# A fused sparse-attention and ELU-MLP kernel: another opening order, earlier phase starts, and a later first local pair

## The chip, the core and the metric

The kernel runs on one core of a Trainium2 chip. The metric is device time in microseconds (us). The kernel before takes 330.13 us, the median of three runs (329.86 to 330.19). Engines are called PE (TensorE, matrix products and transposes), DVE (VectorE), ACT (ScalarE), POOL (GpSimd, which here mostly issues loads) and SP (SyncE, which issues output and transposing DMAs).

## The reference

Eight batches of eight heads, 576 positions of 64 columns. Heads 0 to 3 see the last 32 positions ("local"), heads 4 to 7 see the earlier positions with the same remainder by 32 ("strided"). The attention output, 4608 rows of 512, goes through two layers with an ELU between them.

```python
rel = pos[:, None] - pos[None, :]
mask_local = (rel >= 0) & (rel < 32)
mask_strided = (rel >= 0) & (pos[None, :] % 32 == pos[:, None] % 32)
scores = np.where(masks, q @ k.T / sqrt(64), -1e9)
attn = softmax(scores); x = attn @ v
h = x @ w_in                       # 512 -> 2048
g = np.where(h > 0, h, np.exp(np.minimum(h, 0)) - 1)
out = g @ w_out                    # 2048 -> 512
```

## The kernel before

**Staging.** Batch 0's attention is computed first, alone: the opening. Then come nine phases, `nb` = 0 to 8. Phase `nb` runs the MLP on chunk `nb` (512 rows) and, woven into it in phases 0 to 6, the attention of batch `nb + 1`. A phase has 16 slots `s`; each makes one 128-wide block of the first layer (`moe_in`, four 128x512 matmuls at L609), its activation (`moe_act`: an exponential on ACT at L635 into e_sb, then two DVE steps at L642 and L644 into g_sb), and one part of the second layer (`moe_out`, four matmuls at L654). Four parts make one output tile; the last copies the bank to o_sb on ACT (L658) and SP sends it out. From phase 1 on all these tiles share a single PSUM bank, so the first part of a tile can only start once o_sb of the tile before has been copied. A chunk's first three parts run in the last slots of its own phase, the other thirteen in the next one.

**Attention.** A batch has four pairs of heads: s0, s1 strided and l0, l1 local. A pair goes through `t_q` and `t_k` (q and k transposed on PE, L360 or L374, and copied out on ACT, L363 or L377; from batch 3, for local pairs from batch 4, by DMA instead), `scores(0)` and `scores(1)` (L491, for later batches L454; the exponential at L499, or L460 and L474, on ACT into pr; the mask on DVE at L506, or L462 and L477), `av(0)` and `av(1)` (pr times v at L526, divided on DVE at L534 and L535 into x), and `x_out` (x transposed on PE at L562 or L575 and copied into xT on ACT, or DVE for late local pairs, L569, L571, L579; a DMA for local pairs from batch 4). `v_in` (L413) copies a strided v into its layout, `halo` (L419) copies 32 rows of every local v block beside the next block, on DVE.

**Order.** The schedule is manual: each engine runs what the program emits, in that order. The opening's order is a written list, OPENING, with names such as `l0.a1` for av(1) of local pair 0; each `sN` step emits the scores, their exponential and their mask together. ON_VECTOR names the copies of batch 0 that go to DVE, the others go to ACT. Its last entries, `moe.2 moe.3 moe.0 moe.1`, are chunk 0's first three first-layer blocks, one contraction chunk after another (chunks 2 and 3 are the strided pairs). In the phases, TIMES gives per batch the first half-slot of pair 0, the pitch between pairs in half-slots, and the offsets of a pair's pieces from its own start; `attention` makes the table, and the slot loop runs the pieces that are due. Batches from 4 on take the local pairs first. In their phases (`late`) a slot's activation is emitted behind the pieces of its second half. PSUM banks come from rings: three single banks for transposes and AV results, two or three for first-layer blocks, a pair of banks for scores.

**Loads.** POOL issues them as a list: batch 0, w_in in four quarters, batch 1 between these, w_out, then later batches when buffers come free.

The slot loop's core (the lines that set what stands ahead of what on ACT):

```python
run(gaps, (2 * s,) if s else range(-10, 1))
late = EARLY <= nb + 1
if nb < n_chunks:
    moe_in(nb, s)
if nb < n_chunks and not late:
    moe_act(nb, s)
run(gaps, (2 * s + 1,) if s + 1 < MC else range(2 * s + 1, 1000))
if nb < n_chunks and late:
    moe_act(nb, s)
...
for chunk, i in outs(nb, s):
    moe_out(chunk, i)
```

## Time and profile before

| what | us |
|---|---|
| timed runs, median of 3 | 330.13 |
| the profiled execution | 333.11 |
| its span | 331.2 |
| PE busy in the span | 305.3 |
| DVE busy | 243.3 |
| ACT busy | 176.2 |
| POOL busy | 132.2 |

Durations in the text come from the profiled execution. 1.9 us of the execution lie around its span. By the order in time the opening lasts to about 29 us, phase 0 to about 58 and phase 1 to about 96; phases 2 to 6 take some 32 each, phases 7 and 8, without attention, less, and from 314 on there are only the last parts of the second layer. A row such as `164.98 1.02 PE L654 MATMUL ... x4 [0.44 <-ACT o_sb L658]` reads: start, duration, engine, line, operation, count, and in brackets how long the engine had stood idle and what released it. Line numbers are those of the kernel before.

### The profile page before, as it was taken

Reading aid. Unit: us, or ns where it says so; the run is one execution under the profiler, and the core shown is the slowest. Engines: PE = TensorE matmul, PEld = TensorE weight load, DVE = VectorE, ACT = ScalarE, POOL = GpSimd, SP = SyncE. Lnnn points to the kernel's source line nnn. Section 1 sums busy time; section 2 is a strip of 40 time slices with the busy share of each in tenths; the row PEclk is TensorE's granted clock in tenths of the full one; section 3 lists DMA queues with packets and bytes.
Section 4 is the critical chain, followed back from the end, with each engine's and each line's share of the span. In section 5 each row is a group of like instructions: output and inputs, shape, how many; then the busy total and the mean of one; then the engine's idle time right before and its main releaser. Section 6 shows DMA issues by size and latency. Waiting matters only on the chain.

```text
span 331.2 us, 6066 instructions
## 1 busy us (share of the span) xinstructions
PE 305.3 (92%) x2198; PEld 152.7 (46%) x2238; DVE 243.3 (73%) x540; ACT 176.2 (53%) x336; POOL 132.2 (40%) x208
## 2 busy tenths in 40 slices
PE   1787889999999999999999999999999999999992
PEld 1553554455544454445444444444445444444440
DVE  7584688788778878888788878887988566766600
ACT  3744787667545654556544555555455544344320
POOL 9859737857089479819921930000000000000000
PEclk9999699999999999999999999999999999999998
DMA  6999999999999999999989992920110000100012
GB/s 110 152 175 138 182 207 109 135 145 129 131 135 114 115 173 145 141 177 144 136 127 160 163 110 63 144 85 35 49 49 34 33 34 32 63 33 35 32 65 70
DMA packets 102138, 35.67 MB, mean 108 GB/s; under 512 B 79885, under 2 KB 97493, under 8 KB 102101
## 3 DMA queue, kind: packets, MB, share of 16 engines
q0 software_dynamic: 67632, 18.10, 60.0%
q1 hardware_dynamic: 34469, 17.11, 25.7%
q8 instruction: 19, 0.31, 0.4%
q14 instruction: 18, 0.15, 0.1%
HBM read 36.70 MB, written 9.44 MB: 139 GB/s over the span
## 4 chain that ended last, share of the span: by engine, by line
PE 80%; ACT 7%; DVE 5%; issue 3%; DMA 2%; POOL 2%; ACTq 0%; POOLq 0%; DVEq 0%
PE single L654 35%; PE half L609 27%; PE single L609 8%; PE single L526 3%; ACT e_sb L635 2%; DMA k_loc<-in_k_dram 2%; PE pair_a L454 2%; DVE g_sb L644 1%; PE single L374 1%; ACT xT L569 1%; PE single L562 1%; ACT pr L499 1%; ACT o_sb L658 1%; DVE e_sb L642 1%; PE pair_a L491 1%
## 5 line engine op out<-in xcount | busy, mean ns | idle before, releaser
L654 PE MATMUL single<-w_out_sb,g_sb 128*128 128x512 bf16 x559 | 143.6, 379 | 4.0 <-ACT o_sb L658 2.0
L609 PE MATMUL half<-xT,w_in_sb 128*128 128x512 bf16 x419 | 112.9, 387 | 1.4 <-issue 0.7
L635 ACT ACTIVATE e_sb<-half 128x512 f32<-128x512 f32 x109 | 65.6, 602 | 70.6 <-PE half L609 67.4
L642 DVE TENSOR_SCALAR e_sb<-e_sb 128x512 bf16<-128x512 f32 x139 | 61.7, 444 | 40.7 <-ACT e_sb L635 39.8
L654 PEld LDWEIGHTS <-g_sb 128*128 128x128 bf16 x576 | 53.4, 98 | 63.0 <-issue 3.4
L609 PEld LDWEIGHTS <-w_in_sb 128*128 128x128 bf16 x576 | 52.9, 100 | 57.6 <-issue 4.1
L644 DVE TENSOR_TENSOR g_sb<-e_sb,half 128x512 bf16<-128x512 bf16 x104 | 71.6, 688 | 3.6
L609 PE MATMUL single<-xT,w_in_sb 128*128 128x512 bf16 x134 | 36.8, 390 | 0.7 <-issue 0.5
L635 ACT ACTIVATE e_sb<-single 128x512 f32<-128x512 f32 x35 | 21.2, 605 | 20.6 <-PE single L609 18.9
L658 ACT COPY o_sb<-single 128x512 f32<-128x512 f32 x36 | 21.3, 591 | 16.9 <-PE single L654 16.4
L526 PEld LDWEIGHTS <-pr 128*128 128x128 bf16 (+3 forms) x352 | 21.3, 109 | 15.7 <-issue 3.2
L460 ACT ACTIVATE pr<-pair_a 126x936 bf16<-126x936 f32 (+1 forms) x20 | 19.2, 961 | 15.8 <-PE single L454 15.8
L177 POOL DMA_DIRECT2D v_raw<-in_v_dram x32 | 20.5, 685 | 17.9 <-DVE v_str L413 17.9
L177 POOL DMA_DIRECT2D k_str<-in_k_dram x32 | 20.1, 650 | 16.2 <-DMA k_loc<-in_k_dram 6.8
L644 DVE TENSOR_TENSOR g_sb<-e_sb,single 128x512 bf16<-128x512 bf16 x35 | 24.1, 688 | 1.2
L177 POOL DMA_DIRECT2D q_str<-in_q_dram x28 | 18.1, 675 | 6.0 <-DMA w_in_sb<-in_moe_w_in_dram 1.9
L535 DVE TENSOR_TENSOR x_l<-single,rden 96x384 bf16<-96x384 f32 x32 | 17.7, 554 | 1.1
L535 DVE TENSOR_TENSOR x_s<-single,rden 126x256 bf16<-126x256 f32 (+1 forms) x32 | 15.7, 491 | 1.1
L499 ACT ACTIVATE pr<-pair_a 128x576 bf16<-128x576 f32 (+2 forms) x20 | 13.0, 652 | 5.3 <-PE pair_a L491 5.2
L534 DVE RECIPROCAL rden<-single 96x6 f32<-96x6 f32 (+2 forms) x64 | 11.9, 185 | 2.8 <-PE single L526 2.4
L569 ACT COPY xT<-single 128x540 bf16<-128x540 bf16 x16 | 9.7, 608 | 7.1 <-PE single L562 7.1
L200 POOL DMA_DIRECT2D q_loc<-in_q_dram x16 | 12.5, 805 | 1.7 <-DMA v_raw<-in_v_dram 0.8
(111 smaller groups left out, 264.0 us busy)
## 6 DMA issues: line engine op xcount, KB each, us to landing
out_dram<-o_sb SPq DMA_DIRECT2D x36, 256.0 KB, 2.2
v_loc<-in_v_dram POOLq DMA_DIRECT2D x8, 288.0 KB, 8.6
k_str<-in_k_dram POOLq DMA_DIRECT2D x32, 67.5 KB, 4.4
v_raw<-in_v_dram POOLq DMA_DIRECT2D x32, 67.5 KB, 5.0
w_in_sb<-in_moe_w_in_dram POOLq DMA_DIRECT2D x4, 512.0 KB, 9.5
w_out_sb<-in_moe_w_out_dram POOLq DMA_DIRECT2D x4, 512.0 KB, 15.2
q_str<-in_q_dram POOLq DMA_DIRECT2D x28, 67.5 KB, 8.3
q_loc<-in_q_dram POOLq DMA_DIRECT2D x4, 288.0 KB, 5.7
```

The costliest lines, as they stand in the source:

```text
L177: engine.dma_start(out=t[0:108, h].rearrange("p g d -> p (g d)"), in_=rows[h, :, 0:30, :].rearrange("t (r g) d -> t r (g d)", g=5))
L460: nc.scalar.activation(both, sc[0:nk, :, 0:w], ACT.Exp, scale=scale)
L499: nc.scalar.activation(halves, sc[0:nk, :, 0:w], ACT.Exp, scale=scale)
L526: nc.tensor.matmul(av[0:m, p, blk - b0, :], lhsT=pr[0:nk, o:o + m], rhs=vt[0:nk, 2 * self.hp + p, blk, :], start=True, stop=True)
L535: nc.vector.tensor_tensor(self.x[0:nq, b0:b0 + n].rearrange("q g p d -> q p g d"), av[0:nq, :, 0:n, 0:D], r.unsqueeze(3).to_broadcast([nq, ...
L569: copy(rows[:, :, 0:30].rearrange("d t (r g) -> d t r g", g=5), groups[:, :, 0:108].rearrange("d g (t r) -> d t r g", r=6))
L609: nc.tensor.matmul(hps, lhsT=w_in_sb[:, c, m * 128:(m + 1) * 128], rhs=xT[:, c, nb * N_TILE:(nb + 1) * N_TILE], start=start, stop=stop)
L635: nc.scalar.activation(e_sb, hps, ACT.Exp)
L642: nc.vector.tensor_scalar(e1_sb, e_sb, scalar1=1.0, scalar2=1.0, op0=ALU.min, op1=ALU.subtract)
L644: nc.vector.tensor_tensor(g_of[nb][:, m, :], e1_sb, hps, op=ALU.max)
L654: nc.tensor.matmul(ops, lhsT=g_of[nb][:, m, kk * 128:(kk + 1) * 128], rhs=w_out_sb[:, m, :], start=(m == 0), stop=(m == MC - 1))
L658: nc.scalar.copy(o_sb, ops)
```

## The change

1. The opening list has another order. Masks are steps of their own (`m0`, `m1`), so a mask can stand behind other DVE work. The v copies stand ahead of the first local mask, the local scores ahead of the strided AVs, `moe.2` inside the local AVs, and q's transposes of batch 1's strided pairs (`S0.t_q`, `S1.t_q`) among the last steps; phase 0 leaves these two out.
2. Batch 0's halo copy goes from DVE to ACT.
3. Strided v of batch 1 is loaded ahead of its local q.
4. Batch 1 starts at half-slot 3 and not 4, batch 2 at 4 and not 6.
5. From batch 4 on, pair 0 (local) starts at half-slot 2 and not 1, with its av(1) where it was; the other pairs stay.
6. In late phases the last slot's activation is emitted ahead of the pieces left over.

```diff
-    (4, 6, (-3, -2, 0, 2, 4, 6, 9, 3)),
-    (6, 6, (-3, -2, 0, 2, 4, 6, 8, 0)),
+    (3, 6, (-3, -2, 0, 2, 4, 6, 9, 3)),
+    (4, 6, (-3, -2, 0, 2, 4, 6, 8, 0)),
     (2, 7, PIECES),
-    (1, 7, PIECES),
+    ((2, 8, 15, 22), 0, PIECES),
...
-s0.cast_q s0.t_q s0.t_k s1.cast_q s1.t_k s0.s0 s1.t_q s0.s1 l0.t_q s1.s1 s1.s0 l0.t_k
-l1.t_q l0.s0 s0.v l1.t_k s1.a0 s0.a0 l0.s1 s1.a1 s0.a1 l1.s0 l1.s1 s1.x s0.x s1.halo
-l0.a0 l0.a1 l1.a0 l1.a1 l0.x moe.2 l1.x moe.3 moe.0 moe.1
+s0.cast_q s0.t_q s0.t_k s1.cast_q s1.t_k s0.s0 s0.m0 s1.t_q s0.s1 s0.m1 l0.t_q s1.s1
+s1.m1 s1.s0 s1.m0 l0.t_k l1.t_q s0.v l0.s0 l0.m0 l1.t_k l0.s1 s1.a0 s0.a0 l0.m1 l1.s0
+s1.a1 s0.a1 l1.s1 l1.m0 s1.halo s1.x s0.x l1.m1 l0.a0 l0.a1
+l1.a0 moe.2 l1.a1 S0.t_q l0.x S1.t_q moe.3 l1.x moe.0 moe.1
...
     load_strided(1, "k")
+    load_strided(1, "v")
     load_local(1, "q")
-    load_strided(1, "v")
...
-                nc.vector.tensor_copy(t[0:32, :, 1:6, 0:D], t[96:128, :, 0:5, 0:D])
+                copy = nc.vector.tensor_copy if self.b else nc.scalar.copy
+                copy(t[0:32, :, 1:6, 0:D], t[96:128, :, 0:5, 0:D])
...
+            if self.b:
+                self.mask(u)
+        def mask(self, u):
...
+        begin = start if b >= EARLY else [start + pitch * i for i in range(4)]
         if b >= EARLY:
-            gaps[start] = [pairs[3].halo]
+            gaps[begin[0]] = [pairs[3].halo]
...
+            if b == 1 and pr.strided:
+                pr.t_q = lambda: None
...
-                               (at[5], lambda pr=pr: pr.av(1)),
+                               (at[5] - (b >= EARLY and i == 0),
+                                lambda pr=pr: pr.av(1)),
...
-                gaps.setdefault(start + pitch * i + off, []).append(piece)
+                gaps.setdefault(begin[i] + off, []).append(piece)
...
+    pairs.update((f"S{hp}", Pair(1, True, hp)) for hp in range(2))
...
-            late = EARLY <= nb + 1
+            late = EARLY <= nb + 1 and s + 1 < MC
```

More of the change, by code (lines that the diff above doesn't have):

```diff
@@ L499, in scores @@
             nc.scalar.activation(halves, sc[0:nk, :, 0:w], ACT.Exp, scale=scale)
+            self.pr[u] = pr
+            if self.b:
+                self.mask(u)
+        def mask(self, u):
+            nk, nq = self.blocks(u)[0][4:]
+            w = len(self.blocks(u)) // 2 * nq
+            halves = self.pr[u][0:nk, 0:2 * w].rearrange("k (a x) -> k a x", a=2)
             if not self.strided:
@@ L508, in scores @@
                                     op=ALU.mult)
-            self.pr[u] = pr
         def av(self, u):
@@ L545, in step @@
             elif what[1:].isdigit():
-                (self.scores if what[0] == "s" else self.av)(int(what[1:]))
+                {"s": self.scores, "m": self.mask, "a": self.av}[what[0]](int(what[1:]))
             else:
```

## The prediction

> **What bounds the kernel now.** I read the page's busy table first (TensorE, PE, is busy 92% of the span, no other engine over 73%), then PE's table of waits, then the order in time around each wait, and last PE's busy time in short windows with the clock that it was granted.

> ```profile
> PE single L360 <- ACT q_str L347: 3.6, 1, 3.6
> PE single L274 <- DVE key_q L272: 2.7, 1, 2.7
> PE single L654 <- ACT o_sb L658: 2.0, 5, 0.4
> PE pair_a L491 <- ACT kT_str L363: 1.1, 1, 1.1
> PE pair_a L491 <- ACT pr L499: 1.0, 2, 0.7
> ...
> PE single L374 <- ACT xT L571: 0.7, 2, 0.4
> ...
> PE single L575 <- DVE x_l L535: 0.7, 2, 0.5
> ```

> Columns: total us, times, longest. The first two are the first loads and the mask set-up, which the change leaves alone. Taken by window, all the rest but some 3 us lies before 58 us; from 58 us on PE hardly stops, and what it still waits for is one 0.51 at 93.96 and five waits for o_sb. So the end is set by PE; a wait of PE that goes shortens the run by its own length unless another takes its place.

> The late o_sb waits are one pattern, at 132.92, 164.98, 197.03 and 229.08, one for each of phases 3 to 6. PE, then ScalarE (ACT), start and duration in us:

> ```profile
> 162.64 1.04 PE L654 MATMUL single<-w_out_sb,g_sb 128*128 128x512 bf16 x4
> 163.51 1.03 PE L609 MATMUL half<-xT,w_in_sb 128*128 128x512 bf16 x4
> 164.98 1.02 PE L654 MATMUL single<-w_out_sb,g_sb 128*128 128x512 bf16 x4 [0.44 <-ACT o_sb L658]
> ```
> ```profile
> 162.70 0.97 ACT L460 ACTIVATE pr<-pair_a 128x960 bf16<-128x960 f32 x1 [0.85 <-PE single L454]
> 163.57 0.39 ACT L474 ACTIVATE pr<-single 128x96 bf16<-128x96 f32 x2
> 163.83 0.62 ACT L635 ACTIVATE e_sb<-single 128x512 f32<-128x512 f32 x1
> 164.31 0.62 ACT L658 COPY o_sb<-single 128x512 f32<-128x512 f32 x1
> ```

> The product that ends about 163.6 has its bank copied only at 164.31, because the exponentials of the local pair and an e_sb stand ahead of it. There is one such bank, so the next product stands still.

> The opening is different: PE is slow there as well as waiting. From the chain:

> ```profile
> 26.83 0.85 PE half L609 x2
> ...
> 57.47 0.86 PE single L654 x4
> ```

> Two 128x512 matmuls take as long as four do later: half pace until about 28.99. The clock column reads 1.00 there, but the pitch decides. It then reads 1.00 to about 32.4, 0.50 to about 39.2, and 1.00 after.

> **The change part by part.** The order of the changed program holds the same matmuls, copies and loads; they are moved, and one copy changes engine.

> *Late phases.* The first local pair's scores go behind the product whose bank is the only one. Replayed at phase 4: the first-layer matmuls end at 162.18, the product runs 162.18 to 163.05 and its last result is there at 163.2. ACT has e_sb until 163.0, so o_sb runs 163.25 to 163.85. Scores (0.4) and the next first layer (0.86) put the next product at 164.36: no wait, and 0.51 in hand. What is late next is the pair's chain: exponentials 163.75 to 165.0, masks on VectorE (DVE) to 165.6, its first AV product, also put later, due at 166.1. Slack 0.5. The last e_sb of each phase also passes ahead of the xT copies: they then end at 161.6, and the fourth matmul that reads them comes at 161.97; slack 0.35. On SP one 1.22 us transpose goes behind an output DMA; its result is read a phase later. So 4 x 0.44 = **-1.76**. Bounds: -2.2 (with the 0.1 holes near the scores) and 0.

> *Phase 1.* Batch 2 starts one slot (two half-slots, about 2 us) earlier, so its last transposes stand behind a product and not right behind the DVE that feeds them: **-0.51**. The cover is the loads: v of batch 2 has its last issue about 56.5 and lands 3.7 later, 60.2. Its copy on DVE now comes at 65.14; a slot earlier, and with 2.3 gained above it, 60.6. k lands about 56.5 and is due about 57.6. Cost 0, but every further gain above is paid back there, first as idle DVE. I keep +0.2 for it, bounds 0 and +1.

> *Opening, batch 0.* The v copies pass ahead of the first local mask, but they can't start before v has landed: last issue 9.32 plus 6.1, 15.4; the first AV goes from 16.25 to about 15.85. Local scores 1 pass ahead of the AVs, so ACT's last exponential ends about 18.85 and not 19.74. The halo copy leaves DVE (0.49, 20.64 to 21.13) for ACT, where no row of before has it. ACT's v_str rows take 0.62 for 512 and 0.83 for 768 columns; the line through both gives 1.28 for its 1280. Bounds 0.83 and 1.45, their sum. It waits for v_loc (landed 18.55), which costs nothing now, and ends 20.1 where DVE's ended 21.13. Behind it on ACT stand the four strided xT copies, at 0.7 a pair: 20.8 and 21.5 where they ended 20.4 and 21.1. Local AV 2 and 3 wait for those banks, so the 1.0 gained at the halo shrinks to about 0.6 at local AV 3 (21.5).

> *Opening, q of batch 1.* Ten transposes and two ACT copies of 0.68 come forward into the stretch where ACT waits 4.17 us (24.5 to 28.6). q's loads, last issue 15.9, landing 6.5 to 8.0 later, are in by 22.4 to 23.9; the first use is about 23.5. On PE they stand ahead of products that were back to back and cost 2 x 0.55 at half pace. From 21.85, 12 dense products at 0.43, these 1.1, two local transposes of 0.48 and an AV of 0.36 are 7.6, so the stretch ends at about 29.4 where it ended 29.25. The opening itself gains nothing.

> What follows it does. Before:

> ```profile
> 28.64 0.60 ACT L635 ACTIVATE e_sb<-half 128x512 f32<-128x512 f32 x1 [4.17 <-PE half L609]
> 29.57 0.68 ACT L363 COPY qT_str<-single 128x630 bf16<-128x630 bf16 x1 [0.33 <-PE single L360]
> 30.15 0.69 ACT L363 COPY kT_str<-single 128x630 bf16<-128x630 bf16 x1
> ...
> 33.82 0.60 ACT L635 ACTIVATE e_sb<-half 128x512 f32<-128x512 f32 x1 [0.88 <-PE half L609]
> 34.32 1.35 ACT L413 COPY v_str<-v_raw 126x512 bf16<-126x512 bf16 x2
> ```

> Without the q copy the k copy ends at 30.35, not 30.84, and the scores and all behind them move 0.5. The v copies now stand ahead of the e_sb that waited 0.88 for PE: they start about 32.4, not 34.32, and the AV that waits for them about 33.1, not 34.98: **-1.9**, carried on because PE is the slow one to 39 us. From 39 to 57 us PE waits 0.39, 0.16, 0.30, 0.34 and 0.16; the half-slot earlier start and the xT copies behind a first layer attack these, but DVE is over 90% busy from 40 to 50 us, so I take **-0.4** of the 1.35. Together -2.3, bounds +2 and -3.8.

> *Loads.* v of batch 1 is issued 0.7 earlier, local q 3.1 later (from 23.84 to 26.9, landing 5.7 after at 32.6; first use about 39). POOL holds the same list, so later loads keep their place: 0.

> **Sum** against the profiled execution, 333.11 us with a span of 331.2: -1.76 - 0.51 - 2.3 + 0.2 = -4.4, that is 328.7. The median of the timed runs is 330.13, 2.98 less than the profiled one; I take the same 4.4 off it: **325.7**.

> **The clock.** In windows of 3.41 us the 128x512 matmuls kept PE busy 1.49 (to 25.58: pace stayed half), 3.41 (to 28.99: it rose), 0.54 (to 32.4: it fell), 1.39 (stayed half), 2.44 (rose), 1.57 (stayed full). So it rises somewhere between 1.49 and 2.44, and falls between 1.57 and 0.54. Transposes and short matmuls alone held PE busy 3.07 of the 3.41 us to 11.93, and the pace stayed half. [...]

> **Rivals.**
> - *The clock holds.* In the window to 32.4 the changed order has about 1.14 us of these matmuls, between 0.54 and 1.57. If that is enough, the half-pace stretch goes, and the sixth first-layer block moves by 3.2 and not 1.9: 325.7 - 1.3 = 324.4. Against: the loads of batch 2 then bind. 0.17.
> - *The early gain is lost.* ACT carries halo, xT and q copies in a row; any one late holds PE in order, and DVE may stall for v at 60.2. With nothing left of it, 330.13 - 1.76 - 0.51 = 327.9; at the bad bound, +2, 329.9. 0.18, a third of it at that bound.
> - *The late wait changes place.* The xT copies miss their 0.35 or the masks their 0.5, and each phase pays back 0.44: 325.7 + 1.76 = 327.5. 0.07.
> - *Slower: the clock is late.* The ten transposes split the dense products; if the window that should raise the clock holds under some 2 us of them, PE enters phase 0 at half pace, and there first layers are 5.2 of 9.7 us, 1.8 in 3.41: perhaps too few to rise. A three-slot cycle then takes 9.7 and not 5.7, +4. From about the second cycle (clock still half after 43 us) the run is slower: 330 to 334. Against: by my replay the window to 28.99 holds 2.9. 0.10.
> - Forecast 0.48, by itself 324.8 to 326.8.

> **How the numbers follow.** A measurement of this kernel tells about 0.2%, 0.66 us. Faster: 0.48 + 0.17 + 0.07 + 0.12 of the lost gain = 0.84. Same: 0.05, slower 0.01 of the lost gain; slower 0.10 + 0.01. The range 324.2 to 329.0 leaves out the slow clock and the bad bound.

> **What would show it.** PE's wait for o_sb falls from 2.0 to about 0.2, the 0.51 near 94 is gone; first scores of batch 1 near 30.4 and their AV near 33.1; the halo on ACT about 1.3 long, ending near 20.1, the local AV just behind it. Wrong: a new wait of PE for xT or pr in phases 3 to 6, DVE waiting for v_raw near 60, half clock after 39 us.

## The result, and the profile after

The changed kernel takes **327.56 us** (median of four runs, 326.01 to 327.67) against 330.16 for the kernel before on the same chip; ratio 0.9893, 95% interval 0.9851 to 0.9934. Run again later, it took 327.1 against 331.27 (ratio 0.9892, 0.9854 to 0.993). The medians differ by 2.6 and 4.2 us; both ratios say some 3.5, with an interval of 2.2 to 4.9. The forecast was 325.7, with a range of 324.2 to 329.0: the direction and the range held, and by the first median 1.9 of the 4.4 us that it promised did not come. As 4.4 lies inside the interval, where the forecast failed is to be seen in the parts and not in the whole.

PE's table of waits in the profile of after (span 325.9; its execution took 327.67), the six rows behind its first two (the first loads and the mask set-up, which are as before, 3.7 and 2.7):

```profile
PE single L622 <- DMA w_in_sb<-in_moe_w_in_dram: 1.4, 1, 1.4
PE single L584 <- DVE x_l L544: 0.8, 1, 0.8
PE pair_a L493 <- ACT kT_str L364: 0.8, 1, 0.8
PE pair_a L493 <- ACT pr L501: 0.7, 1, 0.7
PE single L535 <- DVE pr L516: 0.7, 1, 0.7
PE half L622 <- DVE g_sb L657: 0.5, 1, 0.5
```

The wait for o_sb, five times before, is not in the table any more. The first two rows here stand in phase 0 and are new there: weights of the first layer that have not landed, and an x_l that VectorE has not divided. (Lines moved with the change: L622 is the first layer, L667 the second, L671 the copy to o_sb, L493 and L501 the scores and their exponential, L535 the products with v, L584 and L571 the transposes of x.)

Phase 4 around the place where PE stood still for 0.44 us, first PE, then ACT (start and duration in us):

```profile
159.62 1.03 PE L667 MATMUL single<-w_out_sb,g_sb 128*128 128x512 bf16 x4
160.58 0.39 PE L456 MATMUL pair_a<-qT_loc,kT_loc 64*128 64x96 bf16 x10
...
160.94 1.04 PE L622 MATMUL half<-xT,w_in_sb 128*128 128x512 bf16 x4
161.82 1.03 PE L667 MATMUL single<-w_out_sb,g_sb 128*128 128x512 bf16 x4
```
```profile
160.69 0.59 ACT L671 COPY o_sb<-single 128x512 f32<-128x512 f32 x1 [0.27 <-PE single L667]
161.17 0.98 ACT L462 ACTIVATE pr<-pair_a 128x960 bf16<-128x960 f32 x1
```

The copy now runs ahead of the pair's exponentials, right behind its product, and ends at 161.28; the next product comes at 161.82 and waits for nothing. This is the order that the prediction replayed.

The opening and phase 0, PE, from four places in time:

```profile
28.86 0.28 PE L493 MATMUL pair_a<-qT_str,kT_str 64*128 64x126 bf16 x4 [0.78 <-ACT kT_str L364]
...
31.81 0.35 PE L535 MATMUL single<-v_str,pr 126*128 126x65 bf16 x4 [0.69 <-DVE pr L516]
...
42.03 1.04 PE L622 MATMUL single<-xT,w_in_sb 128*128 128x512 bf16 x4 [1.43 <-DMA w_in_sb<-in_moe_w_in_dram]
...
54.60 0.30 PE L584 MATMUL single<-identity,x_l 96*128 96x96 bf16 x3 [0.81 <-DVE x_l L544]
```

The first scores of batch 1 come 2.0 us earlier than before (30.89) and their products with v 3.2 earlier (34.98). But the first o_sb copy comes only 1.5 earlier (58.73 after 60.24). Half of what the opening wins is gone again within phase 0.

A table for the whole text. Each profile is cut at five landmarks; "opening" runs from the first transpose of x_s to the products of batch 1's first pair with v, "phase 0" from there to the first o_sb copy, "phase 1" to the fifth, "rest" to the last. The kernels in the lower rows are those of the experiments.

| kernel | opening | phase 0 | opening + phase 0 | phase 1 | rest |
|---|---|---|---|---|---|
| before | 16.30 | 25.26 | 41.56 | 36.65 | 228.32 |
| late_only | 14.16 | 23.92 | 38.08 | 37.05 | 225.89 |
| early_only | 12.99 | 25.88 | 38.87 | 35.59 | 228.02 |
| after | 13.11 | 26.92 | 40.03 | 36.50 | 225.35 |
| after_again | 13.66 | 25.99 | 39.65 | 35.62 | 225.39 |
| loads_back | 14.06 | 26.73 | 40.79 | 35.59 | 225.45 |
| b2_at6 | 13.00 | 25.62 | 38.62 | 36.58 | 225.58 |
| win2_early | 13.92 | 27.63 | 41.55 | 35.59 | 225.49 |
| sq_back | 13.69 | 26.99 | 40.68 | 35.59 | 226.17 |
| hold | 13.80 | 25.84 | 39.64 | 35.95 | 225.70 |
| b1_at4 | 14.35 | 25.13 | 39.48 | 35.59 | 225.73 |
| b1_at4_win2 | 14.71 | 25.14 | 39.85 | 36.37 | 226.30 |
| halo_dve | 12.09 | 26.21 | 38.30 | 36.48 | 225.34 |
| best | 13.54 | 24.80 | 38.34 | 36.35 | 225.80 |

Two things show how far one profile can be trusted. After, after_again, early_only and b2_at6 run the same program as far as the first o_sb copy, and opening and phase 0 take 38.62 to 40.03 there; the twelve kernels with the late half have 225.34 to 226.30 as "rest". And look at the first two rows: late_only runs the same program as before until phase 3 begins, and yet opening and phase 0 are 3.5 us shorter in its profile. The profile of before, on which the prediction was built, showed the pace at half from 32.4 to 39.2; that of late_only has full pace there. The mean granted clock of every run tells how often: 10 of 66 runs of the kernel before had 0.986 or 0.987 (as the profiled one had) and took 333.2 us in the median; the other 56 had 0.994 or more and took 330.2.

### The profile page after: what moved, and what is told of

Same layout as the page of the kernel before. It is cut to its first block, busy times and chain, and to the rows that moved or that the text cites. A ratio compares the mean times of both kernels' runs of the same rounds, so it can differ in the third digit from the quotient of the medians.

```text
span 325.9 us, 6073 instructions
## 1 busy us (share of the span) xinstructions
PE 302.3 (93%) x2198; PEld 151.5 (46%) x2238; DVE 242.9 (75%) x539; ACT 177.7 (55%) x337; POOL 131.8 (40%) x208
## 3 DMA queue, kind: packets, MB, share of 16 engines
q1 hardware_dynamic: 34469, 17.11, 25.6%
## 4 chain that ended last, share of the span: by engine, by line
PE 77%; DMA 14%; POOL 4%; issue 1%; DVE 1%; ACT 1%; POOLq 0%; DVEq 0%; ACTq 0%
PE single L667 36%; PE half L622 25%; PE single L622 9%; DMA w_out_sb<-in_moe_w_out_dram 6%; DMA q_loc<-in_q_dram 4%; DMA w_in_sb<-in_moe_w_in_dram 3%; PE single L535 3%; PE pair_a L456 2%; DMA v_raw<-in_v_dram 2%; PE single L375 1%; POOL k_str L178 1%; PE single L571 1%; POOL v_raw L178 1%; POOL q_str L178 1%; PE pair_a L493 1%
## 5 line engine op out<-in xcount | busy, mean ns | idle before, releaser
L667 PE MATMUL single<-w_out_sb,g_sb 128*128 128x512 bf16 x557 | 143.4, 379 | 1.5 <-DVE g_sb L657 0.4
L622 PE MATMUL half<-xT,w_in_sb 128*128 128x512 bf16 x420 | 111.3, 382 | 1.7 <-DVE g_sb L657 0.5
L667 PEld LDWEIGHTS <-g_sb 128*128 128x128 bf16 x576 | 53.5, 98 | 59.5 <-DVE g_sb L657 1.0
L622 PEld LDWEIGHTS <-w_in_sb 128*128 128x128 bf16 x576 | 52.2, 99 | 58.1 <-issue 2.2
L622 PE MATMUL single<-xT,w_in_sb 128*128 128x512 bf16 x135 | 36.1, 382 | 2.0 <-DMA w_in_sb<-in_moe_w_in_dram 1.4
L648 ACT ACTIVATE e_sb<-single 128x512 f32<-128x512 f32 x35 | 21.0, 601 | 23.2 <-PE single L622 21.1
L671 ACT COPY o_sb<-single 128x512 f32<-128x512 f32 x36 | 21.2, 588 | 17.7 <-PE single L667 17.1
L535 PEld LDWEIGHTS <-pr 128*128 128x128 bf16 (+3 forms) x352 | 21.5, 108 | 16.7 <-DVE pr L516 1.7
L178 POOL DMA_DIRECT2D q_str<-in_q_dram x28 | 18.2, 695 | 5.6 <-DMA w_out_sb<-in_moe_w_out_dram 2.0
L501 ACT ACTIVATE pr<-pair_a 128x576 bf16<-128x576 f32 (+2 forms) x20 | 13.0, 652 | 5.4 <-PE pair_a L493 5.4
L201 POOL DMA_DIRECT2D k_loc<-in_k_dram x16 | 12.4, 783 | 1.6 <-DMA q_loc<-in_q_dram 1.3
```

Source lines behind the costliest of these rows:

```text
L178: engine.dma_start(out=t[0:108, h].rearrange("p g d -> p (g d)"), in_=rows[h, :, 0:30, :].rearrange("t (r g) d -> t r (g d)", g=5))
L201: nc.gpsimd.dma_start(out=t[:, h // 2, 0:4, h % 2], in_=src[name][b, h, 0:512].rearrange("(i p) d -> p i d", p=128))
L501: nc.scalar.activation(halves, sc[0:nk, :, 0:w], ACT.Exp, scale=scale)
L535: nc.tensor.matmul(av[0:m, p, blk - b0, :], lhsT=pr[0:nk, o:o + m], rhs=vt[0:nk, 2 * self.hp + p, blk, :], start=True, stop=True)
L622: nc.tensor.matmul(hps, lhsT=w_in_sb[:, c, m * 128:(m + 1) * 128], rhs=xT[:, c, nb * N_TILE:(nb + 1) * N_TILE], start=start, stop=stop)
L648: nc.scalar.activation(e_sb, hps, ACT.Exp)
```

## The experiments

Theory A is the prediction's sum: the late half (items 5 and 6 of the change) is worth 1.8 us, the early half (items 1 to 4) 2.6, and they add. Theory B: the early half gives back what it wins, to loads and to chains on VectorE and ScalarE that the earlier start does not move. Theory C: the clock decides, by where its windows fall.

### The two halves: late_only and early_only

late_only is the kernel before with items 5 and 6 alone; early_only is the changed kernel without them:

```diff
-    ((2, 8, 15, 22), 0, PIECES),
+    ((1, 8, 15, 22), 0, PIECES),
...
-                               (at[5] - (b >= EARLY and i == 0),
+                               (at[5],
...
-            late = EARLY <= nb + 1 and s + 1 < MC
+            late = EARLY <= nb + 1
```

> The kernel before with the late phases' part alone (first local pair a half-slot later, last activation ahead of the left-over pieces). Theory: each of phases 3 to 6 loses its whole gap between the starts of two products, 0.61 (164.98 against 164.37), not the 0.44 shown as idle, and the last one also the 0.28 by which a group of four products stretched to 1.30 at 258.33: 4 x 0.61 + 0.28 = 2.7 us less, no wait for o_sb above 0.2. Rival (as predicted): 4 x 0.44 = 1.76 less. Second rival: most of the gain of the whole change is elsewhere, under 1 us less here.

> The whole change without its late part (items 5 and 6 undone). Theory: what is left is the opening and phases 0 and 1, 1.9 us less than before in the profile up to the end of phase 2, with the four waits for o_sb back. Rival: the early part's gain in the one profile came from where the clock's windows fell, and the timed runs show between 0 and 1 us less.

late_only took 329.36 against 330.05 (ratio 0.9959, 0.9921 to 0.9997), early_only 329.16 (0.9954, 0.9923 to 0.9985). The product of the ratios, 0.9913, agrees with the whole change within the intervals: nothing speaks against the halves adding. In late_only five of twelve runs had a granted clock of 0.985 or 0.986 (median 330.8); the seven others, 0.994 to 0.999, took 328.2. In the same comparison the kernel before took 329.9 at such clocks and 333.2 in its five runs at 0.986 or 0.987, so the late half is worth 1.7 and 2.4. early_only is 0.9 less than the kernel before by the medians of all runs and 1.5 by the ratio (0.5 to 2.5); the forecast had 2.6 for it. In early_only's profile the old wait stands in each of phases 3 to 6, at 129.61, 161.67, 193.72 and 225.77; here the second:

```profile
160.20 1.03 PE L622 MATMUL half<-xT,w_in_sb 128*128 128x512 bf16 x4
161.67 1.02 PE L667 MATMUL single<-w_out_sb,g_sb 128*128 128x512 bf16 x4 [0.44 <-ACT o_sb L671]
```

The late half is thus all that it was said to be, and more: "rest" goes from 228.32 to 225.89 in late_only and from 228.02 to 225.35 in after, 2.4 to 2.7 and not 1.76 (1.7 to 3.0 with the spread of "rest" above). The rows show why. Start to start it is 161.67 - 160.20 = 1.47 where such a group without a wait takes 0.86, so each wait cost 0.61; the 0.44 in brackets leaves out the last 0.17 us of the 1.03 for which the group ahead is counted as busy. Four of them are 2.4, as late_only's theory had it. The early half is what came out small.

### Parts of the early half: loads_back and b2_at6

loads_back is the changed kernel with item 3 undone; b2_at6 has batch 2 at half-slot 6 again:

```diff
     load_strided(1, "k")
-    load_strided(1, "v")
     load_local(1, "q")
+    load_strided(1, "v")
```
```diff
-    (4, 6, (-3, -2, 0, 2, 4, 6, 8, 0)),
+    (6, 6, (-3, -2, 0, 2, 4, 6, 8, 0)),
```

> The whole change, with batch 1's loads in the old order (local q ahead of strided v). Theory: the new order makes the last load of w_out wait for local q (1.59 on POOL at 35.77), and with it every later load comes some 3 us late; undone, PE's 1.43 wait for the third quarter of w_in and DVE's 2.8 wait for v of batch 2 go, and the run is 1 to 2 us shorter than with the whole change. Rival: these loads are late because transfers from 25 to 30 us were slow for another reason (the rate there was 74 to 124 GB/s against 140 to 164 before); then both waits stay and the time is the same within 0.5.

> The whole change, with batch 2 started at half-slot 6 as before. Theory: started at 4, DVE stood 2.8 us for v of batch 2 and PE 0.54 behind it; at 6 that wait is under 1 and PE's 0.54 goes, but the 0.5 wait of the last local transposes for DVE at the end of phase 1 comes back, so the time is within 0.7 of the whole change. Rival: the earlier start is worth its 1.3 us (the step of the output copies between the fourth and the fifth), and the run is over 1 us longer.

loads_back took 326.73 (ratio 0.9885, 0.9832 to 0.9939), no different from the changed kernel. The wait for the weights is gone from its profile, and another has come:

```profile
PE single L535 <- ACT v_str L414: 1.4, 1, 1.4
```

So in these two profiles item 3 moves the weights back and v forward by about the same: the two waits change places (1.43 for 1.43). The wait for the weights does not come with the new order each time, though: early_only, sq_back and hold have that order and no such wait. The prediction's 0 for the loads is right as a sum and wrong in its reason ("later loads keep their place"). DMA moved 83 and 105 GB/s in the two halves of the stretch from 27 to 31 us in after and 165 and 128 in loads_back. Over the whole stretch it is 84 to 114 in after, after_again, early_only, b2_at6, win2_early, sq_back and hold, which have both strided loads back to back, and 141 to 154 in before, late_only and loads_back, where a local load stands between them. That the loads behind come later for this reason is a reading; no run singles it out.

b2_at6 took 327.87 (ratio 0.9923, 0.9894 to 0.9953), 0.3 to 0.8 more than the changed kernel, which the intervals alone do not tell apart. Its wait for x_l at the end of phase 1 is 0.5 again, and phase 1 takes 36.58, as before. Of the eleven profiles with batch 2 at 4, seven take 35.59 to 35.95 there. The other four, after, b1_at4_win2, halo_dve and best, take 36.35 to 36.50; in after VectorE waits 2.80 for v of batch 2, in best 2.1. So the step was named rightly and is worth about 1.0, and nearly nothing where v comes late.

b2_at6 also measures the opening and phase 0 by themselves, as beside late_only nothing else differs in it, in one comparison: 327.87 against 329.36, so 1.5 less. Among runs with clocks of 0.994 or more it is only 0.5 (327.7 against 328.2). The rest comes from executions at a low clock: 15 of 78 runs of the two kernels with the old opening had 0.985 to 0.987, but only one of 86 runs of the kernels with a new one. Which of its moves does that isn't shown.

### The clock's windows and single moves: after_again, win2_early, sq_back, hold

win2_early issues the last quarter that phase 0 waits for ahead of batch 1's local loads. sq_back puts batch 1's strided q back into phase 0. hold adds nine products whose results nobody reads, three at each of three idle places:

```diff
+    load_w_in(2)
     load_local(1, "q")
...
-    load_w_in(2)
```
```diff
-l1.a0 moe.2 l1.a1 S0.t_q l0.x S1.t_q moe.3 l1.x moe.0 moe.1
+l1.a0 moe.2 l1.a1 l0.x moe.3 l1.x moe.0 moe.1
...
-            if b == 1 and pr.strided:
-                pr.t_q = lambda: None
```
```diff
+    def fill(n, bank):
+        for _ in range(n):
+            nc.tensor.matmul(bank, lhsT=w_in_sb[:, 0, 0:128], rhs=w_in_sb[:, 0, 0:512],
+                             start=True, stop=True)
...
+            if (self.b, self.name) == (1, "s0"):
+                fill(3, coming())
...
+            if (self.b, self.name, u) == (1, "s0", 0):
+                fill(3, coming())
```

> The changed kernel once more, beside the next three on one chip. The theory that the two halves of the change add: late half -1.9, early half -0.9, so 327.3 against 330.1 and a ratio near 0.992. The rival that the halves help each other (the first run of the changed kernel, 327.56, by luck on the slow side): 326.5 or less. In its profile the late half should show at every late phase again (the start of the copy of the late products 0.6 earlier per phase), and the opening may come out up to 1.5 us otherwise than in the first profile, since the transfers of its first 30 us do not land alike in two executions.

> The last load of the first weights (the one that the products at 42.03 waited 1.43 us for) is issued ahead of the local loads of batch 1 instead of behind them; nothing else differs from the changed kernel. Theory that the load order cost the early half its gain: the wait of 1.43 goes, the local loads of batch 1 land some 2 us later and are used late enough, so -1.0 to -1.4 us against the changed kernel of the same call. Rival: the time comes back at the next wait in line (the activation of the half, 0.54 at 66, or the local values of batch 1, which the run with the old load order waited 1.4 for): within 0.5 of the changed kernel. Slower by up to 1 would mean that the local loads of batch 1 were the tighter ones.

> The transposes of batch 1's strided q go back to phase 0; the rest is the changed kernel's, the order of the opening too. In the changed kernel's first profile these ten transposes took 0.53 us of TensorE's time at 23.9 to 25.3 and lay in the window that ended at 25.14 with 3.12 of 3.41 us busy, after which the granted clock was 1. Theory that all of TensorE's busy time counts in that window: without them it holds some 2.6, the clock rises one window later, at 28.5, and the nine dense products of the opening that ran in 0.4 to 0.6 us take 0.63; the first scores of batch 1 come 1 to 1.5 us later than 28.86, and the two heads' transposes fall into idle time of phase 0 (0.78 at 28.1, 0.69 at 29.1), which gives some 0.5 back: +0.5 to +1 us in all. Rival, the reading of the prediction that only the dense products count: the rise stays where it is and the kernel is the same or up to 0.5 faster, as the transposes then lie in idle time.

> Nine products of 128x512 whose results nobody reads are added, three each ahead of the first two scores and of the first products with the values of batch 1, where TensorE stood idle for 0.78, 0.69 and 0.69 us in the window from 28.56 to 31.97 (1.68 us busy, after which the granted clock fell to half for one window of 3.41 us). At full clock three take some 0.66 us of TensorE. Theory that the busy share of that window decides: with them it holds some 3.4, the clock stays, and the 3.41 us of work at half clock that followed take 1.7 less; the added products cost at most 0.3 where they outlast the idle time: -1.0 to -1.5 against the changed kernel of the same call. Rival: the work behind that point is bound by its loads (the wait of 1.43 at 42.03 for the weights grows by what is gained), so the time is the same within 0.4 and the wait for the weights shows 2.5 to 3. Third: the clock falls as before whatever is added, and the nine products cost up to 0.7.

In one comparison: after_again, the changed kernel once more, 327.1, win2_early 327.83, sq_back 328.18, hold 327.69, against 331.27 (ratios 0.9892, 0.9905, 0.9918 and 0.9902, each about 0.004 either way). None of the other three is faster than the changed kernel. The two theories of after_again, 327.3 where the halves add and 326.5 or less where they help each other, are too near for it to tell.

- *win2_early.* The wait for the weights is gone, and nothing is won: as the rival had it, the time comes back at the next wait, though not at one that it named. Phase 0 takes 27.63. The transposes of x_s now wait 1.06 for VectorE, and the window of 3.41 us that holds this idle time (2.05 busy) is followed by one at half pace, from about 44.6:

```profile
43.66 0.32 PE L571 MATMUL single<-identity,x_s 108*128 108x108 bf16 x3 [1.06 <-DVE x_s L544]
...
44.29 1.57 PE L622 MATMUL half<-xT,w_in_sb 128*128 128x512 bf16 x4
```

- *sq_back.* About 1 us slower by the median, as expected, and for another reason: the clock did not rise late (the dense products moved up into the place of the transposes, and the window to 25.6 was full, 3.41 us), but ACT had to copy q and k in a row, and the first scores of batch 1 waited 1.58 for kT_str, not 0.78. The move of these ten transposes into the opening is thus worth about 1, if the difference is real: the intervals of the two ratios overlap.
- *hold.* It tells nothing of the clock: after_again, which has no added products, kept full pace through the same place, where its windows cut the three idle times differently (2.48 and 2.40 us busy, where the first profile had 2.94 and 1.68). What the added products cost, if anything, lies within the 0.6 by which the two differ.

### The earlier start and the halo: b1_at4, b1_at4_win2, halo_dve

```diff
-    (3, 6, (-3, -2, 0, 2, 4, 6, 9, 3)),
+    (4, 6, (-3, -2, 0, 2, 4, 6, 9, 3)),
```
```diff
-                copy = nc.vector.tensor_copy if self.b else nc.scalar.copy
+                copy = nc.vector.tensor_copy
```

The first is b1_at4; b1_at4_win2 adds win2_early's edit to it; the second is halo_dve.

> Batch 1 starts at half-slot 4 of phase 0 again, as it did before the change, so its pieces stand behind the other half of each slot; the rest is the changed kernel's. Between its first products with the values of batch 1 and the first copy of the late products the changed kernel took 25.99 to 26.92 us in its two profiles, where the kernel with the late half alone took 23.92: the waits there are for the weights (0.95 to 1.43), x_s (0.3 to 0.8), x_l (0.8) and pr (0.3 to 0.5), none of which the kernel before has. Theory that the earlier start itself makes them, since every piece is asked for some 0.9 us sooner than VectorE, ScalarE and the weights can give it: with the old start these waits fall from 2.5 to under 1, the stretch takes about 24.5, and as it begins about 0.9 later the whole comes out 0.3 to 0.8 faster than the changed kernel (326.9 to 327.6), near 326.5. Rival: the earlier start was worth its half-slot and the waits come from elsewhere: 0.5 to 1 slower, near 328.

> The old start of batch 1, and besides the last load of the first weights issued ahead of batch 1's local loads. Theory that the two waits are separate: the wait for the weights is gone and so are those for x_s and x_l; 0 to 0.5 faster than with the old start alone. Rival, that with the old start the weights are in time anyway (they land about 42 and would be asked for at 41.5): within 0.3 of it, or slower by what the local loads then come late (first used about 37).

> The halo copy of batch 0 is made by VectorE as before the change; the rest is the changed kernel's. In all profiles of the changed opening the time from the first x_s transpose to the first dense product is 3.58 to 3.59 us, in the two of the old opening 4.91. Theory that the halo on ScalarE (1.27 us there, 0.49 on VectorE) is where most of that 1.32 comes from: with it on VectorE, TensorE waits some 0.5 for it again and the stretch takes 4.1 to 4.6, +0.3 to +0.8 on the whole if it is carried on. Rival, that the order did it (the exponentials and masks ahead of it): VectorE makes the halo in 0.5 us and ScalarE starts the xT copies 1.2 earlier, the stretch takes 3.2 to 3.6 and the whole is the same or up to 0.4 faster.

b1_at4 took 327.12, b1_at4_win2 327.23, halo_dve 326.47, against 330.92 (ratios 0.9877, 0.9882, 0.9877; 0.005 either way). b1_at4 shows what its theory said of the waits: those for the weights, for x_s (0.2 left) and for x_l are gone, phase 0 takes 25.13. (Waits for pr, which it counted too, are no mark of the earlier start: late_only has 1.2 of them, b1_at4 1.0.) But v is waited for 1.33, PE is busy for 1.43 of the 3.41 us to 32.81, and after that the pace is half. All six timed runs seem to have that stretch (granted clock 0.990 to 0.992 in each): 3.41 us at half clock lower the mean of a span of 325 us by 0.005. Of the 0.008 that this profile's 0.992 is short, 0.003 are left, and where they lie is not shown; in before and after the clock column also falls at the idle end of the span, to 0.50 for the last 1.2 us and to 0.78 for the last 0.9. b1_at4_win2 is the same within the noise: with the old start the weights are in time.

halo_dve goes to the rival: the time from the first x_s transpose to the first dense product is 3.09 with VectorE's copy (3.21 in best, which has it too), 3.58 to 3.89 with ScalarE's, 4.91 before. The order of the opening won that stretch, and the halo's move to ScalarE (1.27 us there) lost some 0.5 of it.

### All that helped together: best

The changed kernel with batch 1 at half-slot 4, the halo on VectorE, and eleven unread products (three, three and five) in the idle times of 0.78, 0.69 and 1.33.

> The changed kernel with batch 1 at half-slot 4, the halo copy of batch 0 on VectorE, and eleven products of 128x512 whose results nobody reads (three ahead of each of the first two scores of batch 1, five ahead of its first products with values), which fill the idle times of 0.78, 0.69 and 1.33 us there. With batch 1 at half-slot 4 alone all six timed runs had a mean granted clock of 0.990 to 0.992, where most runs of the other changed kernels have 0.994 to 0.999, and the profile shows the pace at half from about 32.8 to 36, just behind those idle times. Theory that the idle share of a window sets the pace behind it: with the idle times filled the first layers at 33 and 36 take 1.04 and not 1.91 and 1.18, the runs' clocks are 0.995 or more, and the stretch from the first x_s transpose to the first copy of the late products, 39.48 with batch 1 at half-slot 4 alone, takes 37.0 to 37.6; on the whole 1.5 to 2.3 faster than the changed kernel, 324.8 to 325.6. Rival one: the half pace has another cause and stays, so the clocks are 0.990 to 0.992 again and the time is 326.3 to 327. Rival two: the pace is full and the time is taken back by the loads or by VectorE further on (a wait for the weights of 1 or more near 40, for v of batch 2 near 60): full clocks, but 326 to 327.

It took 326.48 against 330.03 (ratio 0.9883, 0.9835 to 0.9932). Five of six runs had clocks of 0.995 to 0.998. First a row of b1_at4, then three of best:

```profile
33.34 1.91 PE L622 MATMUL half<-xT,w_in_sb 128*128 128x512 bf16 x4
```
```profile
30.32 1.24 PE L128 MATMUL single<-w_in_sb 128*128 128x512 bf16 x5
...
32.11 1.03 PE L638 MATMUL half<-xT,w_in_sb 128*128 128x512 bf16 x4
...
40.63 0.81 PE L638 MATMUL single<-xT,w_in_sb 128*128 128x512 bf16 x3 [1.42 <-DMA w_in_sb<-in_moe_w_in_dram]
```

The added products (L128) fill the idle time, and the first layer at 32.11 takes 1.03, where b1_at4 took 1.91 for the same. With the clocks (five of six runs here, none of six in b1_at4) that agrees with the theory that the idle share sets the pace behind it; the halo differs too between the two. And then the second rival comes in: PE is 2.1 us earlier at the weights (39.21 against 41.34) and waits 1.42 for them; VectorE waits 2.1 for v of batch 2 further on. The stretch from x_s to o_sb takes 38.34, not 37.0 to 37.6. This kernel beats the one before; that it beats the changed one isn't shown, as their intervals overlap almost fully.

## Why the prediction was right, and where it was off

- **Late phases, -1.76: right, sized too small.** The wait for o_sb is gone in all four phases, nothing took its place, and the replay of the order held: it had the two products at 162.18 and 164.36, the profile has them at 159.62 and 161.82, both 2.55 earlier by what was won ahead of them. Measured 2.4 in "rest" of the profiles, up to 2.7, and 1.7 to 2.4 in timed runs at like clocks. The term read the idle time in brackets, 0.44, for the cost of the wait, 0.61. Another 0.27 came once, from item 6 at the end of phase 6: there a group of four second-layer products took 1.30 before, at 258.33, and 1.03 after, as its last one had waited for g_sb inside the group.
- **Phase 1, -0.51 with +0.2 for loads: right, the gain sized too small.** 1.0 by b2_at6 where v is in time. The cost that was named came in four of eleven profiles and took nearly all of that, as in the first one: VectorE waited 2.80 for v of batch 2 near 64, PE 0.54 behind it at 66.23, and phase 1 took 36.50; in after_again VectorE waited 1.6 and PE not at all (35.62).

```profile
64.40 0.32 DVE L414 COPY v_str<-v_raw 126x512 bf16<-126x512 bf16 x1 [2.80 <-DMA v_raw<-in_v_dram]
```

- **Opening.** The halo on ACT took 1.27 (predicted 1.28), but its move, which the prediction counted as a gain of 0.6 to 1.0, lost some 0.5 (halo_dve). First scores were forecast at 30.4 and came at 28.50 to 29.67 in the four profiles of this order, the products with v at 33.1 and came at 31.2 to 32.4: more than forecast, because the clock rose early, at about 25.1 in after and 26.3 in after_again, in a window with ten transposes among the dense products, where the replay had half pace to 29.4. Part of the spread is luck: the first transposes of x_s came anywhere from 18.2 to 19.4 in these four.
- **"Together -2.3": the step that failed.** It has two faults. The -1.9 was "carried on because PE is the slow one to 39 us", and the -0.4 took more off the waits of phase 0. In fact phase 0 takes longer: 25.6 to 26.9 in the four profiles of this order where the same stretch takes 23.9 in late_only, whose start is as late as that of the kernel before. The waits for w_in (0.95 to 1.43), x_l (0.8) and x_s (0.3 to 0.7 each) are what stands in between, and each edit that removed one of them met the next: b1_at4, win2_early, loads_back and best all end within some 0.5 us of the changed kernel by their ratios. early_only has no wait for w_in at all, and its phase 0 takes 25.88 all the same. So the loads of weights and of v and the chains of VectorE and ScalarE set the end of phase 0, and not PE's start into it alone; that is read from which waits replace which, and no single run isolates it. The other fault is that PE was slow to 39 us only in executions such as the profiled one, about one in seven; "the same 4.4" could not be taken off a median of runs without that stretch. Against late_only's profile the new opening has no clear gain at the first o_sb copy (58.07 there; 56.86, 58.01, 58.29 and 58.73 in b2_at6, after_again, early_only and after). In timed runs it is worth 0.5 at like clocks, and 1.5 over all runs, since it hardly ever falls into the slow stretch; the 2.3 was too much by either.
- **Sum.** Late half 1.7 to 2.4, phase 1 between nearly 0 and 1.0, opening and phase 0 0.5 at like clocks and 1.5 over all runs: 2.2 to 4.9, against 3.5 by the ratios (2.6 and 4.2 by the medians). That the sum came as near as it did is partly luck: the late half was put too low and the opening too high. Forecast and "early gain is lost" (327.9) were both partly right; the measured medians, 327.56 and 327.1, lie between them, nearer the second.
- **The clock.** "The clock holds" was partly so: in after the pace fell for one window (31.97 to 35.38) and not two, in after_again and early_only for none. The 1.3 that was put on it doesn't show in after_again: PE waits there for the weights (0.95) and for x_s (0.8) behind it. The slow rival never showed.

What stays open: which of the two, the loads or the chains over VectorE, is the last limit of phase 0 once all the others are removed. The profile with both the weights earlier and batch 1 later (b1_at4_win2) had a stretch at half pace, so that none shows phase 0 with neither. A kernel with the halo on VectorE alone besides the changed order (halo_dve, 326.47) is the simplest candidate for better; its gain over the changed kernel isn't resolved.

## To carry to other kernels

Price a wait by the distance from start to start on the waiting engine, with and without it, not by the idle time shown: here 0.61 for 0.44, four times. Before building on a profile, see how its clock and time stand among the timed runs: a stretch that one execution in seven has (here 3 us) can't be won in the others, and a median hides what is won by not having it. And when a start is moved earlier, list what each later piece needs and when that comes by itself; if loads and other engines' chains don't move, the gain ends at the first of them, and taking that one away shows the next.

## What the runs showed of the hardware

| window, kernel | busy | 128x512 | pace after it |
|---|---|---|---|
| 14.66-18.08, best | 3.42 | 0 | half |
| 22.16-25.58, before | 2.86 | 1.49 | half |
| 20.68-24.09, win2_early | 2.93 | 1.47 | half |
| 21.73-25.14, after | 3.12 | 1.25 | rises |
| 21.49-24.90, best | 3.19 | 1.48 | rises |
| 24.09-27.50, win2_early | 3.41 | 1.49 | rises |
| 28.56-31.97, after | 1.68 | 0.98 | falls |
| 29.40-32.81, b1_at4 | 1.43 | 1.04 | falls |
| 41.16-44.57, win2_early | 2.05 | 0.91 | falls |
| 30.77-34.18, late_only | 1.79 | 1.04 | stays full |
| 38.80-42.21, after | 1.98 | 1.22 | stays full |

The fall in after as the trace has it, with the windows ahead of it and behind it (start and end, length, busy, clock column, DMA share, GB/s):

```profile
25.14:28.56 3.42, 2.94 (x25) 1.00 0.89 96
28.56:31.97 3.41, 1.68 (x17) 1.00 1.03 123
31.97:35.38 3.41, 3.41 (x24) 0.50 1.73 154
```

In the first row transposes and short products kept PE busy for the whole window, and the pace stayed at half. In the next five, beside 1.25 to 1.49 us of long products, it stayed at half where PE was busy for 2.86 and 2.93 in all and rose where that was 3.12, 3.19 and 3.41; the two of win2_early differ by 0.02 in long products and by 0.48 in all. So neither long products alone nor all of the work tells these rows apart, and the rise behind 1.25 lies outside the 1.49 to 2.44 of long products that the prediction read from one profile. The pace fell behind windows with 1.43, 1.68 and 2.05 us busy and stayed full behind 1.79 and 1.98: the three that let it fall had 0.91 to 1.04 of long products, the other two 1.04 and 1.22, and of the two at 1.04 the one that fell was busy for 1.43 in all, the other for 1.79. No run changed one of the two kinds of work alone, so what sets the pace is not shown. The steps did not lie at one place from the start of the program: the rise came at 24.90 in best, 25.14 in after, 25.98 in b1_at4, 26.30 in after_again, 27.50 in win2_early and 27.85 in hold, kernels with nearly one opening, and the three idle times of phase 0 lay in one window in after and in two in after_again. The kernel before took 333.2 us in its ten runs with a clock of 0.986 or 0.987 and 330.2 in the 56 others.

**The first loads did not land alike.** The first transpose of x_s started between 18.1 and 20.0 us in 14 profiles whose program is nearly the same to there, and at 18.24, 18.36, 18.70 and 19.42 in b2_at6, after_again, after and early_only, whose program is the same; the latest four of the 14 (19.0 and more) are those where q_loc was waited for longest (1.0 to 1.4). A difference under 1 us in one pair of profiles says little here.
